# A quarter of one batch's weight products, moved from its gates to behind its scores

## The chip, the cores and the metric

The kernel runs on one core of a Trainium2 chip. The metric is the device time of one execution in microseconds (us); of several runs the median is taken. A core has five engines that run side by side and wait for each other by semaphores: TensorE (matmuls into PSUM, a memory of eight banks), VectorE, ScalarE, GpSimd and SyncE. In the profile they are PE, DVE, ACT, POOL and SP; PEld is TensorE's loading of weights.

## The reference

There are 8 batches of 8 heads, 576 positions and head size 64, and 32 memory slots per head. First comes an attention over the memory slots, then a gated feed-forward block on the heads side by side (512 columns, 1536 hidden):

```python
a = softmax(phi, over positions)            # 576 x 32 per head
k_m, v_m = a^T k, a^T v                     # 32 x 64 per head
attn = softmax(q k_m^T / sqrt(64))          # 576 x 32 per head
x = attn v_m                                # 576 x 512 per batch, heads side by side
g, val = x w_gate, x w_val                  # 576 x 1536
out = (silu(g) * val) w_out                 # 576 x 512
```

## The kernel before, in words

**The algebra.** x is never formed. Since x w_gate = attn (v_m w_gate), the kernel multiplies the small v_m by the weights first. This gives for each batch a matrix U (256 rows of heads and slots, 2 x 1536 columns for gate and value), and the gates multiply the normalised attention A by U. `u_round` (L460) makes the products: for each part that it is handed, it takes two PSUM banks (p_u0 and p_u1, one for each group g of heads), runs 8 matmuls of 512 columns (L472), and after the matmuls of all its parts evacuates every bank into U (t_U), by ScalarE (L492, "a") or VectorE (L496, "v"), as a string of letters says. A part is named by which (0 gate, 1 value) and by the chunk c of 512 hidden columns. So a batch has six parts: gate and value of chunks 0, 1 and 2.

**The stages of a batch.** `scores` (L392) multiplies qT by k_m for a group of heads, 8 matmuls into two banks (p_g, p_v), and ScalarE takes their exp (L407) into t_E. There are two groups. `z_inv_v` and `norm` on VectorE divide by the sums and give A (t_A). Then come the gates: 24 slots, each with two matmuls for the gate into a bank p_g, Silu on ScalarE (L532) into t_sg, two matmuls for the value into a bank p_v, and VectorE's product (L538) into t_h. The products with w_out (`products`, L689; matmuls at L727) are made with fewer multiplications, by sums of blocks of t_h (t_S) and of w_out (t_T); they run in units of two matmuls, of which seven products to a block make the output, and they stand as fillers between the stages of the next batches. Their results are copied (L752) or added (L757) out of PSUM and stored by SyncE.

**What sets the order.** The order of the instructions on every engine is the order in which the program records them; each engine works through its own in order. Stages are laid beside each other by hand, in the gates by `spread` (L852), which sorts items by a place on a scale of 24 slots.

**The banks.** `bank` (L75) takes the first tag of the list `free`, and `done` (L81) puts a tag back at its end as soon as the instruction that reads the bank last is recorded. So a bank is handed on in the order of the program, and whoever gets it waits, on the chip, until that reader has finished.

**Batch 2.** The loop over batches 2 to 7 starts at L996. Batch 2 differs from the others, since the products of batches 0 (`zero`) and 1 (`one`) are filled in by hand. Its order on TensorE is: products of batch 0 mixed with the sums of k and v and the transposes of q; the scores of both groups (L1026); twelve units of batch 0 and six of batch 1 (L1031); the rest of batch 1's products with the normalisation; then `u_three` (L840, called at L1054), a round of three parts, (gate, chunk 0), (value, chunk 0) and (gate, chunk 1); six last units of batch 1; and the gates. The fourth part, (value, chunk 1), is `u_values` (L845): for batch 2 it stands in the gates, between slots 2.5 and 3 (L1068), with both evacuations on ScalarE. Later batches have it behind their scores (L1029). Chunk 2 follows in the gates, beside the next batch's sums (L1077).

**The buffers.** `u_buffer` (L551) places the U of a chunk for both groups under one tag, U0 for chunk 0. Batch 1's block sums t_S of chunk 0 have the same tag (L597), and so U of batch 2, chunk 0, can be written only when the products that read these sums are done.

Of the kernel before, what the change touches and what calls it, by code (L numbers as in the profile page):

```python
# [10 lines left out]
BF16 = mybir.dt.bfloat16  # L11
# [3 lines left out]
def kernel(  # L15
# [40 lines left out]
    att = ctx.enter_context(tc.tile_pool(name="att", bufs=2))  # L56
    upool = ctx.enter_context(tc.tile_pool(name="upool", bufs=1))
# [17 lines left out]
    def bank(shape, dtype, name):  # L75
        tag = free.pop(0)
        t = ps.tile(shape, dtype, tag=tag, name=name)
        held[id(t)] = tag, t
        return t

    def done(*tiles):  # L81

        for t in tiles:
            free.append(held.pop(id(t))[0])
# [29 lines left out]
    def load_qT(b):  # L114

        qTs[b] = att.tile([128, NS, 128], BF16, tag="qT", name="t_qT")
        nc.sync.dma_start_transpose(out=qTs[b], in_=qs[b])
# [8 lines left out]
    HC = CH // 2  # L126
# [16 lines left out]
    def w_part(which, c, i, g, halves):  # L143

        w = W[which, c][64 * g:64 * g + 64]
        h0, h1 = halves[0], halves[-1] + 1
        return w[:, h0:h1, i] if c == 0 else w[:, i, HC * h0:HC * h1]
# [20 lines left out]
    ephis, rSs, bkvs, kTs, es, atts = {}, {}, {}, {}, {}, {}  # L168

    def phi_exp(b):  # L170
        t = att.tile([128, JK, NP, M], BF16, tag="ephi", name="t_ephi")
        nc.scalar.activation(
            out=t.rearrange("p j i m -> p i j m"),
            in_=phis.pop(b).rearrange("p i (j m) -> p i j m", m=M),
            func=AF.Exp,
        )
        ephis[b] = t
# [278 lines left out]
    Us = {}  # L456
# [3 lines left out]
    def u_round(b, parts, evac):  # L460


        banks = []
        for which, c, halves in parts:
            w0, w1, h0, h1 = which[0], which[-1] + 1, halves[0], halves[-1] + 1
            n = (h1 - h0) * HC
            p = [bank([128, CH], FP32, f"p_u{g}") for g in range(NG)]
            for w in which:
                o = (w - w0) * n
                for i in range(NP):  # L470
                    for g in range(NG):
                        nc.tensor.matmul(  # L472
                            p[g][32 * i:32 * i + 32, o:o + n],
                            lhsT=kTs[b][64 * g:64 * g + 64, 2, 32 * i:32 * i + 32],
                            rhs=w_part(w, c, i, g, halves),
                            start=True,
                            stop=True,
                            tile_position=(64 * g, 32 * i),
                        )
            for g in range(NG):  # L480
                if (b, c, g) not in Us:
                    u_buffer(b, c, f"U{c}")
                if len(which) == 1:
                    dst = Us[b, c, g][:, h0:h1, w0]
                else:
                    dst = Us[b, c, g][:, h0]
                src = p[g][:, 0:(w1 - w0) * n].rearrange("p (a f) -> p a f", f=HC)
                banks.append((dst, src, p[g], rSs[b][:, g:g + 1] if b in scaled else None))
        for (t, p, home, r), e in zip(banks, evac):
            if e == "a":  # L490
                if r is None:
                    nc.scalar.copy(out=t, in_=p)  # L492
                else:
                    nc.scalar.activation(out=t, in_=p, func=AF.Copy, scale=r)
            elif r is None:
                nc.vector.tensor_copy(out=t, in_=p)  # L496
            else:
                nc.vector.tensor_scalar(out=t, in0=p, scalar1=r, scalar2=None, op0=ALU.mult)
            done(home)
# [50 lines left out]

    def u_buffer(b, c, tag):  # L551

        t = upool.tile([128, NG, 2, 2, HC], BF16, tag=tag, name="t_U")
        for g in range(NG):
            Us[b, c, g] = t[:, g]
# [86 lines left out]
    def wait_for(x):  # L642

        t = att.tile([1, 1], BF16, tag="mark", bufs=1, name="t_mark")
        nc.gpsimd.tensor_copy(out=t, in_=x)
# [183 lines left out]
    def q_items(b, evac):  # L829
        return [lambda n=n: q_T(b, n, evac[n]) for n in range(3)]  # L830
# [9 lines left out]
    def u_three(b):  # L840

        evac = "avavav" if b in (3, 5) else "avaava"
        u_round(b, (((0,), 0, (0, 1)), ((1,), 0, (0, 1)), ((0,), 1, (0, 1))), evac)

    def u_values(b):  # L845

        u_round(b, (((1,), 1, (0, 1)),), "aa")
    def run(items):
        for x in items:
            x()  # L850
# [10 lines left out]
    def exp_tables():  # L861
        nc.scalar.preload_act_table_set("natural_log_exp_and_others")

    def gv_slots(b):
        return [lambda s=s: gv_slot(b, s) for s in range(2 * NJF)]
# [108 lines left out]
    def take(n):  # L974
        nonlocal backlog
        n = max(0, min(n, len(backlog)))
        part, backlog = backlog[:n], backlog[n:]
        return part
# [3 lines left out]
    def loads(b):  # L982

        if b < B:
            load_q(b)
            load_phi(b, nc.gpsimd)
            load_k(b)
            load_v(b)

    def run_late():  # L990
        run(late)
        late.clear()
# [3 lines left out]
    for b in range(2, B):  # L996
        last = b + 1 == B
        exp_tables()
        if b == 2:
            load_qT(3)  # L1000
            phi_exp(2)
            (zero, ops0), (one, ops1) = products(0, ("c11",)), products(1, ("p1", "c11"))
            kv, q2 = kv_items(2), q_items(2, "aaa")
            run(zero[:6])
            sums = {n: f for n, f in zip(((1, 1), (0, 2), (1, 2)), late)}
            late.clear()
            sums[0, 2]()
            weight_sums(0)
            weight_sums(1)
            run(zero[6:12] + one[:6] + kv[:1] + q2[:2])  # L1010
            weight_sums(2, (0, 1))
            run(zero[12:16] + zero[18:22] + kv[1:] + q2[2:] + zero[16:18] + zero[22:24])
            weight_sums(2, (2, 3))
            ops0["c11"]()
            ops1["p1"]()
            wait_for(Ts[2][0:1, 3, 0, 0:1])
            for part in ((0, 1), (3,), (2,)):
                for c in (1, 2):
                    sums[1, c](part)
            loads(4)  # L1020
            backlog = one[6:12] + zero[36:] + one[12:36]
            ops = ops1
        else:
            run(take(6))
        for g in range(NG):
            scores(b, g)  # L1026
        if b > 2:
            ops["p1"]()
            u_values(b)  # L1029
        else:  # L1030
            run(zero[24:36] + take(6))  # L1031
        run(take(6))
        z_inv_v(b, 0)
        ops["c11"]()
        run(take(6))
        if not last:
            phi_exp(b + 1)
        z_inv_v(b, 1)
        if b > 2:
            norm(b, 0)  # L1040
            norm(b, 1)
        run(take(6))
        run_late()
        if b == 4:
            wait_for(atts[4, 1][0:1, 0, 0:1])
            quad_sums(0)
        nc.scalar.preload_act_table_set("silu_and_others")
        run(take(6))
        if b == 2:
            norm(2, 0)  # L1050
        run(take(6))
        if b == 2:
            norm(2, 1)
            u_three(2)  # L1054
            run(one[36:])
        g = gv_slots(b)
        quad = []
        if b == 4:
            quad = products(b, (), 0)[0]
        if last:  # L1060
            rest, rest_ops = products(b, (), 1)
            backlog += rest[:12]
        beside = 0 if last else 2 if quad else min(4, len(backlog))
        outs = [lambda: run(take(1)) for _ in range(len(backlog) - beside)]
        streams = [(g, 0, 24), (quad[:12], 0, 3), (quad[12:], 12, 18.5)]
        streams += [(outs, 4, 7 if quad else 24)]
        if b == 2:
            streams += [([lambda: u_values(2)], 2.5, 3)]  # L1068
        if last:
            streams += [([u_item(b, 2)], 5, 6)]  # L1070
        if not last:
            if b > 2:
                load_qT(b + 1)
            if b > 2 and b != 4:
                phi_sum(b + 1)
            streams += [
                (kv_items(b + 1, lambda: (u_item(b, 2, "aava")(), run(take(2)))), KV, KV + 4),  # L1077
                ([lambda: (u_three(b + 1), run(take(2)))], 19, 20),
            ]
        spread(*streams)  # L1080
        flush_mul()
        units, ops = products(b, ("p1", "c11"))
        backlog += units
# [34 lines left out]
```

## Time and profile before

| | |
|---|---|
| median of 3 runs | 233.97 us (233.71 to 234.56) |
| span of the profiled execution, first to last instruction | 231.4 us |
| the profiled execution's own time | not recorded apart from its span |
| TensorE busy | 221.6 us |
| VectorE / ScalarE / GpSimd busy | 185.1 / 171.7 / 140.8 us |
| mean granted TensorE clock | 0.997 of full speed |
| a pair of gate matmuls (128x288) to the next pair, in batch 2 | 0.245 us |
| evacuation of a p_u bank (128x512), ScalarE / VectorE | 0.59 / 0.68 us |

In the lines of the profile, L is a line of the kernel, `out<-in` the tiles written and read, x the number of instructions; behind the bar stand busy time and mean length, then the idle time before. A line of the chain of waits has the start, the length and the work in it. In a timeline a line has the start, the length, the engine and the work; square brackets hold the engine's idle time before it and what ended it. Instructions of one engine overlap by a little, so that a start may lie before the end of the one ahead.

### The profile page before, as it was taken

The numbers are of one execution on the slowest core, as the hardware profiler recorded it, in microseconds if no ns is written. First come the engines' busy times: TensorE is split into PE (matmuls) and PEld (weight loads), VectorE is DVE, ScalarE is ACT, GpSimd is POOL, SyncE is SP. The second block draws the span as 40 slices with busy tenths as digits, with TensorE's granted clock in tenths as the row PEclk, the third lists the DMA queues.
The fourth block names the chain that finished last, engine by engine and source line by source line (L and its number), as shares of the span: only waits on it lengthen the run. The fifth ranks groups of instructions, "written<-read, shape, count | busy, mean of one in ns | idle before, by whom it ended". The sixth has DMA issues, their size and how long they took to land.

```text
span 231.4 us, 7210 instructions
## 1 busy us (share of the span) xinstructions
PE 221.6 (96%) x2825; PEld 169.8 (73%) x2825; DVE 185.1 (80%) x423; ACT 171.7 (74%) x365; POOL 140.8 (61%) x190
## 2 busy tenths in 40 slices
PE   6987799999999999999999999999999999999993
PEld 2544476778887777878788787887788778878882
DVE  4245789999966799989997668998999899977732
ACT  2777898988447989968896658978898789677310
POOL 8422427998199049765977689464845394039291
PEclk9999999999999999999999999999999999999998
DMA  6999999999996992999299946994014502202125
GB/s 214 210 211 206 199 207 207 221 245 268 205 225 175 256 256 49 223 204 184 71 223 191 226 134 115 252 236 89 28 65 114 104 0 95 91 10 84 31 85 160
DMA packets 36674, 36.84 MB, mean 159 GB/s; under 512 B 14624, under 2 KB 31008, under 8 KB 36640
## 3 DMA queue, kind: packets, MB, share of 16 engines
q0 software_dynamic: 16272, 22.42, 52.5%
q1 hardware_dynamic: 19600, 13.18, 22.9%
q10 hardware_dynamic: 768, 0.79, 1.1%
q8 instruction: 22, 0.36, 0.6%
q14 instruction: 12, 0.10, 0.1%
HBM read 42.47 MB, written 9.44 MB: 224 GB/s over the span
## 4 chain that ended last, share of the span: by engine, by line
PE 86%; DMA 9%; POOL 2%; ACT 1%; issue 0%; DVE 0%; POOLq 0%
PE p_g L515 21%; PE p_os L727 21%; PE p_v L515 20%; PE p_oc L727 10%; DMA W<-in_moe_w_val_dram 9%; PE p_oa L727 5%; PE p_u L472 5%; PE p_kv L230 2%; PE p_g L396 1%; POOL t_kv L99 1%; POOL t_kv L103 1%; PE p_q L383 0%; POOL t_q L108 0%; ACT t_qT L337 0%; POOL W L138 0%
## 5 line engine op out<-in xcount | busy, mean ns | idle before, releaser
L538 DVE TENSOR_TENSOR t_h<-t_sg,p_v 128x288 bf16<-128x288 bf16 x192 | 81.8, 451 | 14.1 <-PE p_v L515 7.0
L515 PEld LDWEIGHTS <-t_U 128*128 128x128 bf16 x768 | 73.9, 98 | 21.2 <-issue 3.5
L532 ACT ACTIVATE t_sg<-p_g 128x288 bf16<-128x288 f32 x192 | 73.3, 424 | 17.1 <-PE p_g L515 11.4
L515 PE MATMUL p_g<-t_A,t_U 128*128 128x288 bf16 x384 | 77.0, 286 | 0.0
L515 PE MATMUL p_v<-t_A,t_U 128*128 128x288 bf16 x384 | 77.0, 286 | 0.0
L727 PEld LDWEIGHTS <-t_S 128*128 128x128 bf16 x384 | 37.5, 98 | 4.5 <-issue 0.2
L603 POOL TENSOR_TENSOR t_S<-t_h 128x512 bf16<-128x512 bf16 x17 | 19.7, 1157 | 32.7 <-DVE t_h L538 31.2
L727 PEld LDWEIGHTS <-t_h 128*128 128x128 bf16 x288 | 27.1, 98 | 8.6 <-issue 5.0
L492 ACT CAST t_U<-p_u 128x512 bf16<-128x512 f32 x51 | 27.0, 605 | 6.6 <-PE p_u L472 6.6
L727 PE MATMUL p_os<-t_T,t_S 128*128 128x256 bf16 x192 | 23.7, 273 | 0.0
L560 POOL TENSOR_TENSOR t_S<-t_S,t_h 128x512 bf16<-128x512 bf16 x17 | 19.6, 1156 | 1.3
L560 POOL TENSOR_TENSOR t_S<-t_h 128x512 bf16<-128x512 bf16 x16 | 18.4, 1152 | 0.0
L560 POOL TENSOR_TENSOR t_S<-t_h,t_S 128x512 bf16<-128x512 bf16 x16 | 18.4, 1152 | 0.0
L472 PE MATMUL p_u<-W,t_kT 64*32 64x512 bf16 (+1 forms) x416 | 15.3, 363 | 1.2 <-DMA W<-in_moe_w_gate_dram 0.6
L496 DVE CAST t_U<-p_u 128x512 bf16<-128x512 f32 x21 | 13.6, 683 | 1.9 <-PE p_u L472 1.9
L727 PE MATMUL p_os<-t_T,t_h 128*128 128x256 bf16 x96 | 14.8, 273 | 0.0
L875 PE MATMUL p_warm<-bones 128*128 128x512 bf16 x44 | 12.5, 421 | 1.7 <-DVE bones L897 1.7
L452 DVE TENSOR_TENSOR t_A<-t_E,t_lz 128x576 bf16<-128x576 bf16 x16 | 11.4, 740 | 0.7 <-ACT t_lz L428 0.7
L727 PE MATMUL p_oc<-t_T,t_S 128*128 128x256 bf16 x96 | 11.9, 273 | 0.0
L727 PE MATMUL p_oa<-WO,t_h 128*128 128x256 bf16 x96 | 11.8, 273 | 0.0
L727 PE MATMUL p_oc<-WO,t_S 128*128 128x256 bf16 x96 | 11.8, 272 | 0.1
L727 PE MATMUL p_os<-WO,t_h 128*128 128x256 bf16 x96 | 11.8, 273 | 0.0
(107 smaller groups left out, 308.3 us busy)
## 6 DMA issues: line engine op xcount, KB each, us to landing
out_dram<-t_o SPq DMA_DIRECT2D x11, 512.0 KB, 3.0
t_kv<-in_k_dram POOLq DMA_DIRECT2D x8, 576.0 KB, 10.5
t_q<-in_q_dram POOLq DMA_DIRECT2D x8, 576.0 KB, 8.4
t_kv<-in_v_dram POOLq DMA_DIRECT2D x8, 576.0 KB, 14.7
t_phi<-in_phi_dram POOLq DMA_DIRECT2D x6, 576.0 KB, 8.1
out_dram<-t_o SPq DMA_DIRECT2D x10, 256.0 KB, 4.5
WO<-in_moe_w_out_dram POOLq DMA_DIRECT2D x3, 512.0 KB, 19.2
W<-in_moe_w_gate_dram POOLq DMA_DIRECT2D x2, 512.0 KB, 16.5
```

The lines of the kernel that those rows point to most:

```text
L230: nc.tensor.matmul(p[g][32 * i:32 * i + 32, 0:n], lhsT=phi_of(b, g, j, i), rhs=kvs[b][64 * g:64 * g + 64, w0:w1, i, j * D:(j + 1) * D], st ...
L452: nc.vector.tensor_tensor(out=a, in0=es.pop((b, g)), in1=lzs.pop((b, g)), op=ALU.mult)
L472: nc.tensor.matmul(p[g][32 * i:32 * i + 32, o:o + n], lhsT=kTs[b][64 * g:64 * g + 64, 2, 32 * i:32 * i + 32], rhs=w_part(w, c, i, g, halve ...
L492: nc.scalar.copy(out=t, in_=p)
L496: nc.vector.tensor_copy(out=t, in_=p)
L515: nc.tensor.matmul(p[:, 0:HALF], lhsT=Us[b, c, g][:, o // 2, which, 128 * (o % 2):128 * (o % 2 + 1)], rhs=atts[b, g][:, r], start=(g == 0) ...
L532: nc.scalar.activation(out=sg, in_=gate[:, 0:HALF], func=AF.Silu)
L538: nc.vector.tensor_tensor(out=dst, in0=sg, in1=val[:, 0:HALF], op=ALU.mult)
L560: eng.tensor_tensor(out=out, in0=x, in1=y, op=ALU.subtract)
L603: eng.tensor_tensor(out=t[:, 0], in0=A21, in1=A22, op=ALU.add)
L727: nc.tensor.matmul(mine[home][:, u], lhsT=lhs(c, m, u), rhs=rhs(c, m), start=fresh and u == 0, stop=(k == 5), skip_group_check=u == 1 or n ...
L875: nc.tensor.matmul(p[:, 0:128 * a], lhsT=bones, rhs=x.to_broadcast([128, a, 128]) if a > 1 else bones, start=True, stop=True,)
```

## The change

The part (gate, chunk 0) of batch 2 becomes a round of its own, recorded directly behind the scores, ahead of batch 0's twelve units, with both evacuations on VectorE. The round ahead of the gates, `u_three`, still has three parts; these are now (value, chunk 0), (gate, chunk 1) and (value, chunk 1). The round in the gates is gone. U of batch 2, chunk 0, no longer lies under U0: its half for group 0 takes the place of t_es (a small tile of sums that `phi_sum`, L205, writes for later batches), the half for group 1 a new place, UX. In the program's order on each engine this is all: TensorE has 8 weight loads and 8 matmuls earlier, VectorE two copies more, ScalarE two fewer, and GpSimd and SyncE stand as before.

```diff
     def u_buffer(b, c, tag):
 
+        if (b, c) == (2, 0):
+            half = (128, 2, 2, HC)
+            Us[b, c, 0] = att.tile(list(half), BF16, tag="es", bufs=1, name="t_U")
+            Us[b, c, 1] = upool.tile(list(half), BF16, tag="UX", name="t_U")
+            return
         t = upool.tile([128, NG, 2, 2, HC], BF16, tag=tag, name="t_U")
...
     def u_three(b):
 
         evac = "avavav" if b in (3, 5) else "avaava"
+        if b == 2:
+            u_round(b, (((1,), 0, (0, 1)), ((0,), 1, (0, 1)), ((1,), 1, (0, 1))), evac)
+            return
         u_round(b, (((0,), 0, (0, 1)), ((1,), 0, (0, 1)), ((0,), 1, (0, 1))), evac)
...
             ops["p1"]()
             u_values(b)
         else:
+            u_round(2, (((0,), 0, (0, 1)),), "vv")
             run(zero[24:36] + take(6))
...
         streams += [(outs, 4, 7 if quad else 24)]
-        if b == 2:
-            streams += [([lambda: u_values(2)], 2.5, 3)]
         if last:
```

## The prediction

> **What bounds the kernel now.** I read the page's first part, then the waits of TensorE, then the chain of waits around batch 2's scores, then ScalarE's and TensorE's timelines there. The page:
>
> ```profile
> span 231.4 us, 7210 instructions
> ...
> PE 221.6 (96%) x2825; PEld 169.8 (73%) x2825; DVE 185.1 (80%) x423; ACT 171.7 (74%) x365; POOL 140.8 (61%) x190
> ...
> PE 86%; DMA 9%; POOL 2%; ACT 1%; issue 0%; DVE 0%; POOLq 0%
> ```
>
> TensorE is busy for nearly the whole span and carries 86% of the chain that ends last. Asked for TensorE's waits from 40 us to the end, the trace lists none. Busy alone would not prove it, since matmul ends are modelled, but the starts do: in the gates a pair of matmuls follows a pair every 0.245 us, in the products a matmul follows a matmul every 0.109 us. So from there on, a microsecond in which TensorE stands still is a microsecond of the kernel, unless something later waits anyway; nothing does. The chain around the scores of batch 2 (start, length, what):
>
> ```profile
> 62.25 0.80 ACT t_qT L337
> 63.05 0.50 ACT t_p L752
> 63.55 0.04 issue
> 63.59 1.47 PE p_oc L727 x12
> 65.06 1.31 PE p_os L727 x12
> ...
> 77.73 0.34 PE p_u L472 x8
> 78.08 0.35 PE p_g L515 x2
> ```
>
> Twice ScalarE holds TensorE here: the scores start behind the third copy of qT, and the product behind the scores (p_oc, 63.59) starts behind ScalarE's copy of that bank. Each time TensorE restarts 0.05 us after ScalarE's end (62.25 + 0.80 = 63.05, scores at 63.10; 62.95 + 0.59 = 63.54, product at 63.59). ScalarE's timeline in that stretch:
>
> ```profile
> 62.25 0.80 ACT L337 COPY t_qT<-p_q 128x768 bf16<-128x768 bf16 x1 [1.08 <-PE p_q L383]
> 62.95 0.59 ACT L752 COPY t_p<-p_oc 128x512 f32<-128x512 f32 x1
> 63.43 0.60 ACT L752 COPY t_q<-p_os 128x512 f32<-128x512 f32 x1
> 63.90 0.62 ACT L752 COPY t_p<-p_os 128x512 f32<-128x512 f32 x1
> 64.38 0.45 ACT L407 ACTIVATE t_E<-p_g 128x288 bf16<-128x288 f32 x1
> ```
>
> It runs without a pause from 62.25. The scores are written by 63.54, but their first exp has three copies ahead of it and ends only at 64.38 + 0.45 = 64.83. Before the change nobody on TensorE minds: the products behind the scores use banks that they already hold.
>
> **The change part by part.**
>
> 1. Eight p_u matmuls (one part: gate weights, first chunk) move behind the scores. They need two PSUM banks. The kernel hands out banks from a list, oldest first, and I followed the list through both kernels. At that place five are free, in the order B3, B4, B1, B2, B7 (B7 last, from the addition c11). The scores take B3 and B4 (first group), then B1 and B2 (second), and give them back behind B7. So the moved round gets **B7 and B3**. B7 is read by VectorE's c11 at 62.86 for 0.69, free at 63.55. B3 holds the scores that the exp at 64.38 reads: free at 64.83. The build shows it: the second p_u matmul waits for a count of ScalarE that is just this exp.
>
> 2. The price of that wait. The second wave of scores starts at 63.22 and a wave lasts 0.12 (63.10 to 63.22), so the round could start at 63.34. Its second matmul starts at 64.83 + 0.05 = 64.88 instead. From the start of such a round to the next full-width matmul the gates show 78.01 - 77.67 = 0.34. So the product behind it starts at 64.88 + 0.34 = 65.22 instead of 63.59: **+1.63**. Behind the waiting matmul, in TensorE's order, stand all products up to the gates, and ScalarE, VectorE and the output stores wait for those. The trace shows no p_u round that waits in its middle: the restart lies between the 0.05 above and 0.16 (an early p_u behind a VectorE copy, 25.76 to 25.92); the way out, counted from the last p_u, between 0.31 and 0.41 (the 24 of u_three end that way), where I take the 0.32 of the equal round. The sum so lies between 1.6 and 1.85; I take 1.63, the nearest rows. A lower clock after the pause I leave out: TensorE already pauses 1.27 us from 16.89 in the load phase, and the granted clock of the stretch 13 to 20 us is 1.00.
>
> 3. The round in the gates goes. TensorE's timeline there:
>
> ```profile
> 77.08 0.41 PE L515 MATMUL p_g<-t_A,t_U 128*128 128x288 bf16 x2
> 77.33 0.41 PE L515 MATMUL p_v<-t_A,t_U 128*128 128x288 bf16 x2
> 77.67 0.41 PE L472 MATMUL p_u<-W,t_kT 64*32 64x512 bf16 x8
> 78.01 0.42 PE L515 MATMUL p_g<-t_A,t_U 128*128 128x288 bf16 x2
> ```
>
> Without it the next p_g would start at 77.33 + 0.245 = 77.575, not at 78.01: **-0.43**. Only 0.22 of that is the matmuls themselves (a wave of u_three takes 0.22); the rest is the change of tile shape in and out.
>
> 4. The two evacuations. ScalarE loses two in the gates (1.07 together at 78.14), VectorE gains two (683 ns each by its CAST row) behind the scores. ScalarE's loss gains nothing: TensorE keeps its 0.245 on either side of them. VectorE stands idle for 1.62 before its addition at 65.17. There the copies start at about 65.36 (the last p_u at 64.90, 0.38 for its run, 0.08 to VectorE's start) and, 0.60 apart as at 75.57 and 76.17 and 0.68 long, end at 66.64, while the addition that is queued behind them has its product at 65.06 + 1.63 = 66.69. So they cost nothing. If they slipped, VectorE has 1.76 more idle before the addition at 73.03. ScalarE has less work in the gates and no longer queues weights ahead of t_sg.
>
> 5. u_three still has 24 matmuls in one round; only which part they compute changes. Nothing is added.
>
> 6. Buffers. The gate part's halves go to the place of t_es, whose next writer is batch 3's phi sum, more than 20 us later, and to a new place. The early round need not wait for the old sums in U0 to be read. GpSimd's and SP's instruction orders are the same in both builds, so no load or store is moved past another. GpSimd's sums up to 72.3 do not wait for TensorE and gain 1.6 of slack.
>
> The sum: +1.63 - 0.43 = **+1.20**. The span goes from 231.4 to 232.6. The profiled execution's own time is not recorded beside its span; the median of the runs, 233.97, stands 2.6 above it, and I take that margin as unchanged: 233.97 + 1.20 = 235.17, or **235.2 us**. The 0.5% that a measurement can tell from no change is 1.17 us here, so the forecast lies just beyond it.
>
> [...] The trace: the exp that empties B3 ends 1.5 us after TensorE could start the round, although the list rotates over all eight banks. [...]
>
> **The rivals.**
>
> A (forecast): the bank wait holds TensorE, 235.2. For it: the build's wait and ScalarE's unbroken row. Its own range: the restart and the way out add up to 0.2, and the runs of before lie from 233.71 to 234.56: 234.8 to 235.9.
>
> B (not slower): TensorE does not feel the wait. One mechanism: the first exp is done before 63.34, because the three copies are not in its way. Then the round goes 63.34 to 63.68, which is 0.09 later than 63.59, and the gates give back 0.43: 233.6. Point of decision: an exp ending 1.5 us earlier than in the trace. Against it: ScalarE's order around the exps is the same in both builds, and its work there starts with what TensorE finished before the change's place. Faster by over 0.5% would need nearly 0.9 more from ScalarE's lighter gates, against which the steady 0.245 speaks.
>
> C: the pause is given back later, because TensorE would have waited anyway: 234.0 at most. Against it: no wait of TensorE from 40 us on.
>
> D: a second wait. The first gates now use other banks, emptied by u_three's evacuations. The closest is the fourth p_g, due at about 77.57 in the old time, whose bank VectorE empties by 76.85: 0.7 spare. If one copy (0.68) came too late by its length, 235.9. Nothing in the trace shows such a lag.
>
> **How the numbers follow.** A 0.80: of it 0.54 beyond 1.17 and 0.26 below, since the open bounds of step 2 all add. B 0.11 (0.06 within 0.5%, 0.05 faster). C 0.03, within. D 0.06, slower. Together: slower 0.60, same 0.35, faster 0.05. Leaving out B and C (0.14) and little of the rest, the range is 234.6 to 235.9.
>
> **What would show it.** Right: TensorE idle for about 1.3 us from 63.6, ended by the exp of t_E (L407) at 64.83; the product behind it at about 65.2; no p_u between the first gates; gates starting at 76.35 + 1.63 = 77.98 and the rest 1.2 later to the end. Wrong: the p_u round in one go before 63.7, or a new TensorE wait elsewhere, or the shift shrinking after 80 us.

## The result, and the profile after

The changed kernel takes 234.58 us (median of 11 runs, 234.43 to 235.11) beside 233.71 us for the kernel before: a ratio of 1.0053, 95% interval 1.0041 to 1.0065. It is slower, by about 1.24 us by this ratio. The two medians alone lie 0.87 apart: the median of 11 includes the three earlier runs of the kernel before, 233.97, 233.71 and 234.56, and the other eight have a median of 233.36, which is 1.22 below 234.58. The forecast was +1.20, on the median of those three runs, 233.97. The interval holds 1.005, so whether it lies beyond the 0.5% named in the prediction cannot be told.

The page of the profile after, the same lines as before:

```profile
span 232.7 us, 7209 instructions
...
PE 222.7 (96%) x2825; PEld 170.1 (73%) x2825; DVE 186.2 (80%) x425; ACT 170.9 (73%) x363; POOL 140.8 (61%) x190
...
PE 86%; DMA 9%; POOL 2%; ACT 1%; issue 0%; DVE 0%; POOLq 0%
```

The shares do not tell the two kernels apart: TensorE is still 96% busy and 86% of the chain. The waits do. Asked for TensorE's waits from 40 us on, the trace of before had none; this one has one line (who waits for whom, total, times, longest):

```profile
PE p_u L472 <- ACT t_E L407: 0.9, 1, 0.9
```

Its place, in TensorE's timeline (the first and the last line of the scores are shown). The last line of scores is followed by the round's first matmul, alone, and the other seven come 1.29 us later:

```profile
62.95 0.28 PE L396 MATMUL p_g<-t_qT,t_kT 64*32 64x288 bf16 x1
...
63.10 0.28 PE L396 MATMUL p_v<-t_qT,t_kT 64*32 64x288 bf16 x1
63.44 0.37 PE L472 MATMUL p_u<-W,t_kT 64*32 64x512 bf16 x1
64.73 0.41 PE L472 MATMUL p_u<-W,t_kT 64*32 64x512 bf16 x7 [0.92 <-ACT t_E L407]
65.07 1.16 PE L732 MATMUL p_oc<-WO,t_S 128*128 128x256 bf16 x9
```

And the chain of waits, which now runs through ScalarE's whole queue: the copy of qT, three copies of products, the first exp, and only then the round.

```profile
62.09 0.80 ACT t_qT L337
62.89 0.49 ACT t_p L757
63.38 0.49 ACT t_q L757
63.87 0.49 ACT t_p L757
64.36 0.32 ACT t_E L407
64.69 0.04 issue
64.73 0.41 PE p_u L472 x7
65.14 1.42 PE p_oc L732 x12
```

Before, only the first copy and the next one were in the chain. ScalarE's work up to this exp has not changed; what has changed is that TensorE waits for its end.

Where the time went can be read by following the same matmul through both traces. This execution entered the scores 0.15 earlier (62.95 against 63.10), a difference of the load phase. From there:

| same matmul | before | after | difference, relative to the scores |
|---|---|---|---|
| product behind the scores (p_oc) | 63.59 | 65.07 | +1.63 |
| first gate matmul of batch 2 | 76.35 | 77.83 | +1.63 |
| next batch's scores | 92.48 | 93.53 | +1.20 |
| last p_oc of t_Q in batch 4's gates, from its second matmul | 135.09 | 136.43 | +1.49 |

The lines of before for the start, the gates, the next scores and batch 4:

```profile
63.10 0.28 PE L396 MATMUL p_g<-t_qT,t_kT 64*32 64x288 bf16 x1
...
76.35 0.65 PE L515 MATMUL p_g<-t_A,t_U 128*128 128x288 bf16 x4
...
92.48 0.29 PE L396 MATMUL p_g<-t_qT,t_kT 64*32 64x288 bf16 x1
...
135.09 0.71 PE L727 MATMUL p_oc<-t_T,t_Q 128*128 128x256 bf16 x5
```

So +1.63 arises behind the scores, 0.43 comes back in the gates, and a further 0.29 appears in batch 4, which the prediction did not have. There no engine is waited for. The timeline of after around it:

```profile
135.64 0.41 PE L515 MATMUL p_g<-t_A,t_U 128*128 128x288 bf16 x2
135.89 0.41 PE L515 MATMUL p_v<-t_A,t_U 128*128 128x288 bf16 x2
136.43 0.70 PE L732 MATMUL p_oc<-t_T,t_Q 128*128 128x256 bf16 x5
```

The p_oc should have come at 135.89 + 0.245 = 136.14. The experiments below come back to it.

VectorE took the two copies in its idle time, and the addition queued behind them still had to wait for its product:

```profile
65.19 1.29 DVE L496 CAST t_U<-p_u 128x512 bf16<-128x512 f32 x2 [1.80 <-PE p_u L472]
66.66 0.69 DVE L762 TENSOR_TENSOR t_o<-p_oc,t_q 128x512 f32<-128x512 f32 x1 [0.18 <-PE p_oc L732]
```

### The profile page after: what moved, and what is told of

Same layout as the page of the kernel before. It is cut to its first block, busy times and chain, and to the rows that moved or that the text cites. A ratio compares the mean times of both kernels' runs of the same rounds, so it can differ in the third digit from the quotient of the medians.

```text
span 232.7 us, 7209 instructions
## 1 busy us (share of the span) xinstructions
PE 222.7 (96%) x2825; PEld 170.1 (73%) x2825; DVE 186.2 (80%) x425; ACT 170.9 (73%) x363; POOL 140.8 (61%) x190
## 4 chain that ended last, share of the span: by engine, by line
PE 86%; DMA 9%; POOL 2%; ACT 1%; issue 0%; DVE 0%; POOLq 0%
PE p_g L515 21%; PE p_os L732 21%; PE p_v L515 20%; PE p_oc L732 10%; DMA W<-in_moe_w_val_dram 9%; PE p_oa L732 5%; PE p_u L472 5%; PE p_kv L230 2%; PE p_g L396 1%; POOL t_kv L99 1%; POOL t_kv L103 1%; PE p_q L383 0%; POOL t_q L108 0%; ACT t_p L757 0%; ACT t_qT L337 0%
## 5 line engine op out<-in xcount | busy, mean ns | idle before, releaser
L492 ACT CAST t_U<-p_u 128x512 bf16<-128x512 f32 x49 | 25.9, 606 | 6.6 <-PE p_u L472 6.6
L496 DVE CAST t_U<-p_u 128x512 bf16<-128x512 f32 x23 | 14.9, 683 | 3.7 <-PE p_u L472 3.7
L883 PE MATMUL p_warm<-bones 128*128 128x512 bf16 x44 | 13.4, 444 | 1.7 <-DVE bones L905 1.7
```

The lines of the kernel that those rows point to most:

```text
L883: nc.tensor.matmul(p[:, 0:128 * a], lhsT=bones, rhs=x.to_broadcast([128, a, 128]) if a > 1 else bones, start=True, stop=True,)
```

## The experiments

The theory under test is that of the prediction: the early round is handed a bank that ScalarE's exp has not yet read, and TensorE, working in order, stands still (bank theory). Its rivals: the two copies moved to VectorE hold up the additions queued behind them (VectorE theory), and the round costs its own change of tile shape (shape theory). All edits are to the changed kernel unless said otherwise.

**The exp sooner.** ScalarE's third copy goes behind the exps.

```diff
             ops0["c11"]()
-            ops1["p1"]()
...
             u_round(2, (((0,), 0, (0, 1)),), "vv")
+            ops["p1"]()
```

> The changed kernel with one edit: ScalarE's copy p1 of batch 1 (0.48 us from its start to the next) stands behind the four exps of the scores instead of ahead of them. Bank theory (the early p_u round waits for the exp that reads its second bank, and TensorE with it): that exp ends 0.48 sooner, so TensorE's pause and the time shrink by 0.48: from 1.24 above the kernel before to about 0.76 above it, ratio 1.0033. VectorE theory (the two copies queued ahead of VectorE's additions cost the time) and shape theory (the round's own change of tile shape costs it): no change against the changed kernel, 1.0053.

Measured: 234.03 us, ratio 1.0018 (1.0007 to 1.0028). TensorE's timeline of this kernel:

```profile
63.70 0.37 PE L472 MATMUL p_u<-W,t_kT 64*32 64x512 bf16 x1
64.49 0.41 PE L472 MATMUL p_u<-W,t_kT 64*32 64x512 bf16 x7 [0.42 <-ACT t_E L407]
```

The pause falls from 0.92 to 0.42, the 0.5 by which the exp comes sooner. The rivals, which expected no change, are out for at least this part. The ratio lies below the 1.0033 by more than its interval. The trace does not: counted from the scores of batch 2 (63.20), the p_oc in batch 4's gates (135.90) stands 0.71 later than before, where the forecast was 0.76 with the gates' saving in it; the end of the span (232.2 beside 231.4) stands 0.7 later, counted in the same way. Some of the difference may be the pause of 0.29 in batch 4, which this profile does not have.

**The bank whose exp is last.** No engine's work is reordered; the list only hands out another bank.

```diff
+            free.insert(1, free.pop(free.index("B2")))
             u_round(2, (((0,), 0, (0, 1)),), "vv")
```

> The changed kernel with one edit: the second bank handed to the early round is the one whose exp is the last of four instead of the first. No engine's order of work changes. Bank theory: the last exp ends 0.88 to 0.90 later than the first (64.36 and 65.27 are the starts in the profile of before less 0.02, three steps of 0.30), so the pause and the time grow by 0.89: about 2.1 above the kernel before, ratio 1.0091. VectorE theory and shape theory: no change against the changed kernel, 1.0053, or little.

Measured: 236.84 us, ratio 1.0139 (1.0122 to 1.0156). The direction is right, the size is not: 3.2 us above before instead of 2.1. TensorE's waits and timeline of this kernel:

```profile
PE p_u L472 <- ACT t_E L407: 1.8, 1, 1.8
PE p_oc L732 <- issue: 1.1, 1, 1.1
```

```profile
63.66 0.37 PE L472 MATMUL p_u<-W,t_kT 64*32 64x512 bf16 x1
65.85 0.41 PE L472 MATMUL p_u<-W,t_kT 64*32 64x512 bf16 x7 [1.83 <-ACT t_E L407]
...
137.03 0.41 PE L515 MATMUL p_v<-t_A,t_U 128*128 128x288 bf16 x2
138.50 0.71 PE L732 MATMUL p_oc<-t_T,t_Q 128*128 128x256 bf16 x5 [1.06 <-issue]
```

The pause behind the scores grew as forecast, from 0.92 to 1.83 (0.91, three exps of 0.30). The surplus in this profile is the second line: the same p_oc in batch 4 as in the changed kernel, now 1.2 late, with "issue" as its releaser. Up to there the forecast holds: the p_v ahead of it (137.03, scores from 63.16) stands 2.12 later than before (134.85, scores from 63.10).

**The round one product later.** It gets the same banks, which have been read by then.

```diff
-            u_round(2, (((0,), 0, (0, 1)),), "vv")
-            run(zero[24:36] + take(6))
+            run(zero[24:30])
+            u_round(2, (((0,), 0, (0, 1)),), "vv")
+            run(zero[30:36] + take(6))
```

> The changed kernel with one edit: the early round stands one product (12 matmuls, 1.31 us) later, behind p_oc instead of directly behind the scores. It gets the same two banks, and both are read by then. Bank theory: no pause; the round still changes the tile shape in and out, as it did in the gates, so it costs 0.43 there and saves 0.43 in the gates: the time of the kernel before, ratio 1.000. VectorE theory: the copies still stand ahead of additions, so about 1.2 above the kernel before stays, 1.005.

Measured: 233.52 us, ratio 1.0001 (0.9990 to 1.0012). The round now goes in one piece:

```profile
63.91 1.47 PE L732 MATMUL p_oc<-WO,t_S 128*128 128x256 bf16 x12
65.31 0.41 PE L472 MATMUL p_u<-W,t_kT 64*32 64x512 bf16 x8
65.65 1.48 PE L732 MATMUL p_os<-t_T,t_S 128*128 128x256 bf16 x12
```

The moved round, its buffers and its copies on VectorE are all there, and the loss is gone. What is left is what the round cost in the gates. VectorE theory is out.

**The copies on ScalarE.**

```diff
-            u_round(2, (((0,), 0, (0, 1)),), "vv")
+            u_round(2, (((0,), 0, (0, 1)),), "aa")
```

> The changed kernel with one edit: the early round's two copies are on ScalarE instead of VectorE. Bank theory: TensorE waits for the same exp, so the changed kernel's time, ratio 1.0053. VectorE theory: VectorE has its old work again, so the time of the kernel before less the 0.43 of the gates, 0.998.

Measured: 234.43 us, ratio 1.0039 (1.0027 to 1.0051), with the same pause of 0.92 in its trace and no lateness in batch 4. Bank theory expected 1.0053, VectorE theory 0.998, which the interval excludes; the intervals of this and of the changed kernel overlap. In the trace, counted from the scores (63.09), the p_oc in batch 4's gates (136.29) stands 1.21 later than before.

**The gates' round kept.** The round ahead of the gates loses (value, chunk 1), which goes back into the gates.

```diff
-            u_round(b, (((1,), 0, (0, 1)), ((0,), 1, (0, 1)), ((1,), 1, (0, 1))), evac)
+            u_round(b, (((1,), 0, (0, 1)), ((0,), 1, (0, 1))), "avaa")
...
+        if b == 2:
+            streams += [([lambda: u_values(2)], 2.5, 3)]
```

> The changed kernel with one part undone: the round (value, chunk 1) is back in the gates between slots 2.5 and 3, with its copies on ScalarE, and the round ahead of the gates has two parts. The early round behind the scores stays. By the sums of the prediction the round in the gates costs 0.43 again, and the round ahead of the gates is a wave of 0.22 shorter: 0.21 above the changed kernel, about 1.45 above the kernel before, ratio 1.0062. If the gates' round cost nothing on TensorE: 0.22 below the changed kernel, 1.0044.

Measured: 234.82 us, ratio 1.0063 (1.0051 to 1.0075): the number expected, but partly by luck, as the second of the two timelines below shows. In its gates the round costs what it cost before:

```profile
78.96 0.41 PE L515 MATMUL p_v<-t_A,t_U 128*128 128x288 bf16 x2
79.30 0.41 PE L472 MATMUL p_u<-W,t_kT 64*32 64x512 bf16 x8
79.64 0.42 PE L515 MATMUL p_g<-t_A,t_U 128*128 128x288 bf16 x2
```

That is 79.64 - 78.96 - 0.245 = 0.43. The saving from the shorter round ahead of the gates (16 matmuls, a wave of 0.22 less) did not arrive in this trace, though: the next product then waits 0.25 for VectorE's addition out of its bank.

```profile
75.79 0.63 PE L472 MATMUL p_u<-W,t_kT 64*32 64x512 bf16 x16
76.67 0.60 PE L732 MATMUL p_os<-t_T,t_h 128*128 128x256 bf16 x4 [0.25 <-DVE t_o L762]
```

**The value part joined to chunk 2's round** (an edit to the kernel before, in search of the gates' saving without the early round).

```diff
-            streams += [([lambda: u_values(2)], 2.5, 3)]
...
-                (kv_items(b + 1, lambda: (u_item(b, 2, "aava")(), run(take(2)))), KV, KV + 4),
+                (kv_items(b + 1, lambda: (u_joined() if b == 2 else u_item(b, 2, "aava")(), run(take(2)))), KV, KV + 4),
...
+    def u_joined():
+        u_round(2, (((1,), 1, (0, 1)), ((0,), 2, (0, 1)), ((1,), 2, (0, 1))), "avaava")
```

> The kernel before with one edit: the round (value, chunk 1) leaves its place in the gates and joins chunk 2's round some five slots later, behind the sums of k and v, where the tile shape is changed anyway. No bank there is waited for by the list. Shape theory of the gates' saving: 0.43 goes and a wave of 0.22 comes, so 0.22 below the kernel before, ratio 0.9991. Rival: the value part is now needed about 1.2 us after its matmuls, and two more copies stand in ScalarE's and VectorE's queues there, so TensorE waits for a copy (0.6 to 0.7 each): the same to 0.5 above, 1.000 to 1.002.

Measured: 233.41 us, ratio 1.0006 (0.9994 to 1.0018): no gain. Behind the joined round two value matmuls come late (0.245 would be the step):

```profile
81.50 0.42 PE L515 MATMUL p_g<-t_A,t_U 128*128 128x288 bf16 x2
81.95 0.42 PE L515 MATMUL p_v<-t_A,t_U 128*128 128x288 bf16 x2
82.21 0.41 PE L515 MATMUL p_g<-t_A,t_U 128*128 128x288 bf16 x2
82.55 0.40 PE L515 MATMUL p_v<-t_A,t_U 128*128 128x288 bf16 x2
```

The 0.20 and the 0.10 eat the gain. VectorE's timeline there:

```profile
80.91 0.99 DVE L266 TENSOR_SCALAR t_bkv<-p_kv,t_rS 128x128 bf16<-128x128 f32 x4 [0.34 <-PE p_kv L230]
81.82 1.28 DVE L496 CAST t_U<-p_u 128x512 bf16<-128x512 f32 x2
```

Both late matmuls start 0.05 after VectorE has finished reading a bank (80.91 + 0.99 = 81.90; the first of the two copies, 0.68 long, ends at 82.50). So they probably wait for these banks, of which the joined round takes six at once; the trace names no releaser, and this was not tested. This place does not yield a version faster than both.

**The unexplained pause in batch 4.** Three kernels with one common edit: the warm-up matmuls of the load phase are cut into narrower ones, which puts 204 more instructions ahead of everything else in TensorE's stream and leaves the work behind as it is.

```diff
-    warm(104)
+    warm(104, 104)
...
-    warm(8)
+    warm(8, 8)
...
-    warm(4)
+    warm(4, 4)
...
-    warm(8)
+    warm(8, 8)
...
-    warm(12)
+    warm(12, 12)
```

> The late-bank kernel (e2), whose profile has a second TensorE pause of 1.1 us in batch 4's gates, at 137.4, that no engine's wait explains, with one edit far from it: the warm-up matmuls of the load phase are issued as 102 narrow ones more, of the same total width, so that 204 instructions more (weight loads and matmuls) stand ahead of everything else in TensorE's stream. Fetch theory (that pause is TensorE waiting for its own instructions, whose transfer comes late there): the place of the pause is bound to a position in the stream, so it goes from that matmul, and 1.0 to 1.2 us go: about 2.3 above the shifted kernel before (e9). Data theory (the pause comes from the bank handed out or from batch 4's sums): the pause stays at the same matmul, 3.2 above.

> The changed kernel with the same 102 more narrow warm-up matmuls. Its profile has 0.28 us of that unexplained pause at 136.3. Fetch theory: the 0.28 goes from that matmul, and the time is 1.2 above the shifted kernel before (1.64 for the pause behind the scores less 0.43 in the gates). Data theory: 0.28 stays.

> The kernel before with the same 102 more narrow warm-up matmuls: the control for the two others. TensorE waits for loads in that phase anyway, so no theory expects a change there beyond the 0.3 that the load phase varies by between runs: ratio 0.999 to 1.002, and no pause in batch 4's gates.

Measured: the shifted kernel before, 233.59 us, 1.0006 (0.9997 to 1.0014), the control. The shifted changed kernel, 234.84 us, 1.0072 (1.0049 to 1.0094): 1.25 above the control, as expected (one of its six runs, the profiled one with 236.57, was granted 0.58 of the clock from 27.10 to 28.70 us, in the load phase already, so the median is compared here and not the ratio). The shifted late-bank kernel, 237.34 us, 1.0158 (1.0140 to 1.0176): 3.75 above the control, which neither theory expected. In the shifted late-bank kernel's trace the pause at that p_oc is gone:

```profile
139.27 0.41 PE L515 MATMUL p_v<-t_A,t_U 128*128 128x288 bf16 x2
139.51 0.71 PE L732 MATMUL p_oc<-t_T,t_Q 128*128 128x256 bf16 x5
```

The fetch theory forecast that, the data theory did not. By itself it decides little, since the same p_oc is also on time in unshifted profiles: in the kernel before (134.85 + 0.245 = 135.095, start at 135.09) and with the copies on ScalarE (136.04 + 0.245 = 136.285, start at 136.29). The records of the queue that the profile calls instruction (q8) add to it. Its last transfer ahead of this p_oc ended at 133.51 in the kernel before, 1.58 ahead of the p_oc, which was on time; in the changed kernel at 135.09, 1.05 ahead of the time at which the p_oc was due, and it came 1.34 after that end, 0.29 late. In the late-bank kernel a transfer began in the window 135.9 to 137.2 and took 1.19 (5.7% of 16 engines over 1.30), so that it ended at 137.09 or later, less than 0.2 ahead of the due 137.275; the p_oc came 1.23 late. So the pause went with a late transfer of that queue in the two profiles that have it, and was gone in one profile with 204 more instructions ahead. That TensorE waited there for its own instructions is an estimate from these numbers; no view names what it waited for. What took the time instead stands in the same kernel's table by stretches (stretch and length, busy time of PE, PEld, DVE, ACT and POOL, then the granted clock of TensorE, DMA share, GB/s) and in its timeline:

```profile
63.00:66.50 3.50, 1.60 (x31) 0.87 (x28) 1.14 (x3) 3.34 (x8) 2.81 (x4) 1.00 1.23 195
66.50:70.50 4.00, 4.00 (x27) 2.76 (x22) 1.98 (x3) 0.00 (x0) 3.92 (x4) 0.57 0.69 128
70.50:74.00 3.50, 3.50 (x34) 3.14 (x33) 2.70 (x5) 0.15 (x1) 3.50 (x5) 1.00 0.40 150
```

```profile
66.39 0.41 PE L472 MATMUL p_u<-W,t_kT 64*32 64x512 bf16 x7 [1.83 <-ACT t_E L407]
66.73 2.46 PE L732 MATMUL p_oc<-WO,t_S 128*128 128x256 bf16 x12
```

After a pause of 1.83 TensorE was granted 0.57 of its clock on the mean of the 4.00 us from 66.50: twelve product matmuls took 2.46 instead of 1.47, and the stretch lost some 1.7 in all (0.43 of 4.00). The forecast of 2.3 plus 1.7 is 4.0, near the 3.75 measured. In the profile of the unshifted late-bank kernel the clock stayed at 1.00 in the same stretch and the pause in batch 4 was there; of its four other runs three have a mean clock of 0.990 to 0.993, one 0.997. A clock of 0.57 for 4.00 of some 235 us would lower the mean by 0.007. So its surplus over the forecast probably has two causes, each in some executions; a trace is there for one of the five.

## Why the prediction was right

- **What bounds the kernel**: right. Nothing absorbed the loss; from the scores of batch 2 on, each step of TensorE stayed in the time to the end, and rival C (given back later) did not happen.
- **Step 1, the bank**: right. The round's second matmul waited for the exp of t_E, shown by the wait after, by the pause shrinking when that exp comes sooner, growing when another bank is handed out, and vanishing when the round stands one product later.
- **Step 2, +1.63**: measured +1.63 in the profile. The restart came 0.05 after the exp (64.36 + 0.32 = 64.68, restart at 64.73) and the product 0.34 after the restart (65.07), the rows chosen. The upper bounds were read from rows of another kind: the trace puts the wait that ends at 25.92 down to a load of weights, and the 0.41 behind u_three probably holds a wait for an addition (step 5). One reading was wrong, at no cost to the sum: the round could not start at 63.34, since by step 1 its first bank is read by VectorE's addition until 63.55. In the profile after, its first matmul follows that addition (62.70 + 0.68 = 63.38, matmul at 63.44). So rival B was worked out about 0.25 too low: without the exp's wait the round would have cost 0.34 and the gates given back 0.43, which is close to no change.
- **Step 3, -0.43**: measured -0.43 in the profile, and 0.43 again where the round was put back.
- **Step 4, VectorE's copies at no cost**: right; they ran in its idle time, and with the copies on ScalarE the loss stayed.
- **Step 5**: right for the change itself. There was hardly any margin there: already in the kernel before, the product behind u_three starts 0.06 after the addition that empties its bank (74.30 + 0.68 = 74.98, product at 75.04), and with a wave less TensorE waited for that addition at once.
- **The size**: +1.20 against 1.24 by the ratio. The profiled execution also has 0.29 of the pause in batch 4, which the sum did not have, and whether it is usual in the changed kernel one profile cannot tell. Where a profile with the same wait lacks that pause, the sum fits best: at the p_oc in batch 4 the copies on ScalarE are 1.21 later than before, counted from the scores. The time forecast, 235.2, was 0.6 above the median measured, 234.58: the three runs it was added to were slower than the eight later ones (medians 233.97 and 233.36).
- **The clock left out in step 2**: right for this pause of 0.92 (1.00 from 62 to 70 us), but not a safe assumption: after the pause of 1.83 the shifted late-bank kernel had 0.57, the unshifted one 1.00.
- **Rival D** (a second wait in the first gates): did not happen; the gates kept 0.245.

## What to carry to other kernels

When work is moved to a "free" place in the queue of an engine that works in order, as TensorE did here (the product behind the waiting round came 1.63 later with it), look up which buffer it will be handed and who reads that buffer last: a pool that rotates oldest first protects only as far as its readers keep pace, and here the reader had three other copies ahead of it and ended at 64.68, when the round had begun at 63.44. ScalarE's backlog cost nothing until something on TensorE came to depend on its end; waiting one product longer cost nothing either (ratio 1.0001), but then nothing was gained. Measure a forced wait by lengthening and shortening it, not only by removing it.

## What the runs showed of the hardware

- TensorE paused with no engine to blame: 0.29 in the changed kernel and 1.23 in the late-bank kernel, at the same matmul. In both a transfer of the instruction queue had ended late, 1.05 and less than 0.2 ahead of the time at which the matmul was due, beside 1.58 in the kernel before, where it was on time; with 204 instructions more ahead the pause was gone from the late-bank kernel's profile. That queue has 22 transfers, 0.36 MB in all, in the profile before and in the one after; that it brings TensorE's instructions is the author's estimate. The DMA view of the late-bank kernel for the stretch 135.9 to 137.2 holds one of them, ahead of the matmul that comes late at 138.50:

```profile
q8 instruction: 1, 0.02, 5.7%
```

Why this transfer came late was not tested; the 207 packets of queue q1 in the same stretch (52.5%) are one possible reason.

- After a pause of 1.83 us TensorE's granted clock was 0.57 from 66.50 to 70.50 in the shifted late-bank kernel, and 1.00 in the same stretch of the unshifted one, which had the same pause. From 63.00 to 66.50, where the pause lies, TensorE was busy for 1.60 in both. With a pause of 0.9 behind the scores the clock was 1.00 in three profiles: from 62 to 70 us in the changed kernel, and as the mean of the whole execution with the gates' round kept and with the copies on ScalarE. What decides between the two outcomes at 1.83 was not shown.
